# A first transform over 48 rows on quarters of the array, with moved bulk loads, split gate tiles and a new order of work

## The chip, the core and the metric

The kernel runs on one core of a Trainium2 chip. The metric is the device time of one execution in microseconds. The engines are TensorE (PE; PEld is its weight load), VectorE (DVE), ScalarE (ACT), GpSimd (POOL) and SyncE (SP); the last two also issue DMAs.

## The reference, cut to what matters

Three layers in a row. Only the shapes and the steps that the change touches are kept.

```python
x: (8, 3072, 256)                       # batch, sequence, channels
X = np.fft.rfft(x, axis=1)              # over the sequence
Yr = X.real @ w_r - X.imag @ w_i + b_r  # then soft shrinking by 0.01
Yi = X.real @ w_i + X.imag @ w_r + b_i
y = np.fft.irfft(Yr + 1j * Yi, n=3072, axis=1)
...                                     # y as 24576 tokens of 256
logits = y @ phi                        # 32 slots, softmax over all tokens and over the slots
slot_out = mlp_of_8_experts(dispatch.T @ y)
z = combine @ slot_out
...
out = (silu(z @ w_gate) * (z @ w_val)) @ w_out
```

## The kernel before

The program has two phases. Phase 1 is a pipeline over the eight batches, all in one program order; phase 2 is a loop over 576 steps of the gated layer. Between them lies a join: the last batch's logits and slots, the experts' MLP on 32 slots, and the first gate tiles.

**The order.** Phase 1 is a list of tasks. Each `add(engine, fn, ...)` appends a task, with what it reads and writes; `ring` names buffers that take turns. The list `ORDER`, written out by hand, gives the order in which the tasks are emitted: a number is the place of a task in the list, a negative number is the same task given to the second of the two engines that it allows (most often VectorE in place of GpSimd). Each engine works off its own instructions in that order; semaphores between engines, buffers and DMAs are set by the framework. DMAs that SP issues stand in SP's queue in that order too.

**First transform.** A sequence of 3072 is 96 rows (`R1`) times 32 (`R2`). `load_x` brings a quarter of the channels (64) of a batch as a tile "xq" of 96 partitions x 32 x 64, by one DMA on SP; "xq" has two buffers; batch 0 has its own tiles "x0" (`load_first`). `stage_a` takes 16 channels of it: one float32 matmul (L587) of 96 rows x 128 outputs x 512 columns, with the table `fwd` of cosines and sines as weights, into one of two PSUM banks "ac". VectorE turns it by 32 x 32 blocks (L592) into `chan`. There are 16 such matmuls a batch. A float32 matmul shows in the profile as two passes, each with its weight load.

**The rest of a batch.** `stage_c` (L613) does the second step of the transform with the table `cm` (mix), eight passes into a bank "ac", which ScalarE and VectorE split into high and low parts (L629, L632, L635, L638, L647, `sum_lo` L651). `stage_b` (L701) multiplies by the complex weights, `after_b` shrinks (take, gather, relu, `join` L772), `stage_q` (L798) forms the slots' logits on four groups of 32 columns and issues the spreads `yi<-yt` (L827), four DMAs of 64 KB for each of four parts. `logits`, `slots` and `combine` follow, the slots' sums by L1104. `narrow` converts the weights of phase 2 in 18 jobs beside it, through the buffer "cv" (L1202 to L1247).

**The bulk loads.** Near the end of phase 1 `fetch_w1` and `fetch_w2` bring the experts' weights (1 MB for each expert and each matrix) and `fetch_wg` the gate weights into buffers that come free; they stand in SP's or GpSimd's queue among the last spreads. 40 matmuls `hold` (L1391) on an identity fill TensorE while the last logits are made.

**The gate tiles.** `gates(t)` (L1526) multiplies the slots' outputs with a third of w_gate and w_val; `gate_high` (L1532, ScalarE) and `gate_low` (L1537, VectorE) write the high and low parts into one tile `gstk`. `gv(i)` (L1551, L1552) reads 128 columns of it a step; each step has eight matmuls of 512 columns (six of them L1576). `po` (L1464) are the experts' second matmuls.

Of the kernel before, what the change touches and what calls it, by code (L numbers as in the profile page):

```python
# [10 lines left out]
F32 = mybir.dt.float32  # L11
# [21 lines left out]
def dft_tables():  # L33
# [18 lines left out]
    for j in range(NCH):
        for h in range(2):
            if j == 0 and h == 0:
                fwd[:, 0, 0] = 1.0
                fwd[:, 1, 0] = alt1
                for i in range(R2):
                    if i == 0:
                        mix[0, :, j, 0, h, 0] = 1.0
                        continue  # L60
                    src = 0 if i < 16 else 1
# [7 lines left out]
            fwd[:, 2 * h + 1, j] = -np.sin(a)
            a = 2 * np.pi * ((n2[:, None] * (k1[j, h] + 96 * k2)[None, :]) % n) / n  # L70
            mix[2 * h, :, j, 0, h, :] = np.cos(a)
            mix[2 * h + 1, :, j, 0, h, :] = np.sin(a)
            mix[2 * h, :, j, 1, h, :] = -np.sin(a) * sign
            mix[2 * h + 1, :, j, 1, h, :] = np.cos(a) * sign
# [85 lines left out]
for _n, _w in (  # L160
# [11 lines left out]
FWD = 136  # L172
# [191 lines left out]
def kernel(  # L364
# [83 lines left out]
    def phase1():  # L448
# [1251 lines left out]
```

## Time and profile before

| | us |
|---|---|
| median of 3 runs | 1688.4 (1686.91 to 1688.49) |
| the profiled execution | 1691.38 |
| its span in the profile | 1689.5 |

The span is the time from the first to the last instruction of the program in the profile; the execution's own time has 1.9 us around it. "Busy" on TensorE includes the ends of pipelined matmuls, so two neighbours overlap in their records; the distance from start to start tells the pace. "x4" after a line is four passes. In a timeline the brackets hold the idle time of the engine before the group and what ended it. DMA shares and GB/s are those of the 16 DMA engines.

### The profile page before, as it was taken

Reading aid. Unit: us, or ns where it says so; the run is one execution under the profiler, and the core shown is the slowest. Engines: PE = TensorE matmul, PEld = TensorE weight load, DVE = VectorE, ACT = ScalarE, POOL = GpSimd, SP = SyncE. Lnnn points to the kernel's source line nnn. Section 1 sums busy time; section 2 is a strip of 40 time slices with the busy share of each in tenths; the row PEclk is TensorE's granted clock in tenths of the full one; section 3 lists DMA queues with packets and bytes.
Section 4 is the critical chain, followed back from the end, with each engine's and each line's share of the span. In section 5 each row is a group of like instructions: output and inputs, shape, how many; then the busy total and the mean of one; then the engine's idle time right before and its main releaser. Section 6 shows DMA issues by size and latency. Waiting matters only on the chain.

```text
span 1689.5 us, 23317 instructions
## 1 busy us (share of the span) xinstructions
PE 1661.4 (98%) x8186; PEld 1283.0 (76%) x8186; DVE 1307.2 (77%) x2220; ACT 979.2 (58%) x1830; POOL 288.1 (17%) x336
## 2 busy tenths in 40 slices
PE   7999999999999899999999999999999999999998
PEld 4677776776767558888888888888888888888886
DVE  5889888888888458778777777777777777877776
ACT  3655654655656256656666666656656655665564
POOL 1333333334333321100200200200010110110000
PEclk9999999999999999999999999999999999999999
DMA  9477566666658871311310311311231131131111
GB/s 193 93 133 151 106 129 142 124 130 142 127 130 259 283 173 26 81 26 26 81 23 16 81 25 26 74 34 25 44 63 17 22 81 26 25 72 26 25 26 25
DMA packets 260164, 139.94 MB, mean 83 GB/s; under 512 B 210352, under 2 KB 243856, under 8 KB 260048
## 3 DMA queue, kind: packets, MB, share of 16 engines
q1 hardware_dynamic: 249136, 114.47, 32.9%
q0 software_dynamic: 9856, 23.73, 5.6%
q8 instruction: 65, 1.06, 0.3%
q10 hardware_dynamic: 1056, 0.26, 0.1%
q14 instruction: 51, 0.42, 0.1%
HBM read 72.74 MB, written 40.50 MB: 67 GB/s over the span
## 4 chain that ended last, share of the span: by engine, by line
PE 89%; DMA 3%; DVE 3%; SPq 2%; issue 1%; ACT 1%; POOL 0%; ACTq 0%; DVEq 0%; POOLq 0%
PE o L1576 47%; PE pb L701 9%; PE pg L1551 8%; PE pv L1552 8%; PE ac L587 6%; PE ac L613 4%; SPq L827 2%; DMA yi<-yt 1%; PE ch L798 1%; PE ch L866 1%; PE ch L1104 1%; PE ch L1056 1%; PE ch L1012 1%; DMA cm<-in_moe_w_dram 1%; DMA cv<-in_moe_w_val_dram 1%
## 5 line engine op out<-in xcount | busy, mean ns | idle before, releaser
L1576 PE MATMUL o<-hh,wo 128*128 128x512 f32 x2304 | 722.5, 395 | 0.0
L1556 DVE TENSOR_TENSOR h<-sg,pv 128x512 f32<-128x512 f32 x576 | 393.4, 683 | 247.9 <-ACT sg L1554 244.6
L1554 ACT ACTIVATE sg<-pg 128x512 f32<-128x512 f32 x576 | 344.6, 598 | 413.8 <-PE pg L1551 413.8
L1576 PEld LDWEIGHTS o<-hh,wo 128*128 128x128 f32 x2304 | 434.2, 188 | 100.8
L1576 PE MATMUL o<-hl,wo 128*128 128x512 f32 x1152 | 453.8, 394 | 0.0
L1564 DVE TENSOR_TENSOR hl<-h,hh 128x512 fp32r<-128x512 f32 x576 | 397.5, 690 | 0.1
L1563 ACT ACTIVATE hh<-h 128x512 fp32r<-128x512 f32 x576 | 359.4, 624 | 0.3 <-DVE h L1556 0.2
L1576 PEld LDWEIGHTS o<-hl,wo 128*128 128x128 f32 x1152 | 216.1, 188 | 51.9
L1551 PE MATMUL pg<-cst,gstk 96*128 96x512 f32 x576 | 227.7, 395 | 0.0
L1552 PE MATMUL pv<-cst,gstk 96*128 96x512 f32 x576 | 226.1, 393 | 0.6 <-DVE gstk L1537 0.6
L701 PE MATMUL pb<-xg,whl 128*128 128x512 f32 x576 | 183.1, 443 | 1.5 <-ACT yt L753 1.4
L701 PEld LDWEIGHTS pb<-xg,whl 128*128 128x128 f32 x576 | 104.5, 189 | 49.3 <-issue 25.2
L1552 PEld LDWEIGHTS pv<-cst,gstk 96*128 96x128 f32 x576 | 109.7, 190 | 26.0 <-DVE gstk L1537 0.9
L1551 PEld LDWEIGHTS pg<-cst,gstk 96*128 96x128 f32 x576 | 108.1, 188 | 25.6 <-DVE gstk L1537 0.8
L772 POOL TENSOR_TENSOR yt<-r,yt 128x512 f32<-128x512 f32 x68 | 88.5, 1301 | 191.0 <-ACT yt L763 85.0
L592 DVE STREAM_TRANSPOSE chan<-ac 128x512 f32<-128x512 f32 x128 | 90.1, 709 | 34.1 <-PE ac L587 31.5
L587 PE MATMUL ac<-xq,fwd 96*128 96x512 f32 x224 | 111.7, 601 | 1.3 <-DVE sf L638 0.6
L613 PEld LDWEIGHTS ac<-cm,chan 128*128 128x128 f32 x768 | 100.4, 196 | 12.6 <-issue 5.3
L1612 POOL TENSOR_TENSOR e<-e,rs 96x256 f32<-96x256 f32 x28 | 22.6, 833 | 497.8 <-DVE rs L1609 497.8
L613 PE MATMUL ac<-cm,chan 128*128 128x128 f32 x768 | 104.1, 283 | 0.0
L629 ACT ACTIVATE xg<-ac 128x512 fp32r<-128x512 f32 x96 | 56.9, 595 | 59.7 <-PE ac L613 57.5
L701 PE MATMUL pb<-sg,whl 128*128 128x512 f32 x288 | 87.7, 426 | 0.0
(158 smaller groups left out, 1464.8 us busy)
## 6 DMA issues: line engine op xcount, KB each, us to landing
out_dram<-ob SPq DMA_DIRECT2D x190, 128.0 KB, 2.8
yi<-yt SPq DMA_DIRECT2D x368, 64.0 KB, 2.1
xq<-in_x_dram SPq DMA_DIRECT2D x28, 768.0 KB, 8.2
cst<-c_scr POOLq DMA_DIRECT2D x72, 128.0 KB, 2.9
w2s<-in_moe_w_dram POOLq DMA_DIRECT2D x5, 1024.0 KB, 8.4
chan<-in_moe_w_dram SPq DMA_DIRECT2D x7, 512.0 KB, 6.1
x<-in_x_dram SPq DMA_DIRECT2D x4, 768.0 KB, 10.2
cv<-in_moe_w_gate_dram SPq DMA_DIRECT2D x6, 512.0 KB, 4.0
```

The source lines that it names most:

```text
L587: nc.tensor.matmul(out=pt, lhsT=fwd[:, 8 - 8 * dh:136 - 8 * dh], rhs=T[kq][:, :, d1:d1 + 16], start=True, stop=True)
L592: nc.vector.transpose(out=chan[:, 12 * dh:12 * dh + 16, d0:d0 + 16, :].rearrange("p j d i -> p d j i"), in_=T[ka].rearrange("p n d -> p d n"),
L613: nc.tensor.matmul(out=pt[:, :, q:q + 2, i // 2, :], lhsT=chan[:, 16 * dh + j // 2, :, j % 2], rhs=cm[:, j, :].rearrange("p (c h k) -> p c ...
L701: nc.tensor.matmul(out=pt, lhsT=w[:, dh, m, es], rhs=xx, start=m != 1 and dh == 0 and n == 0, stop=dh == 1 and n == 2, skip_group_check=True,)
L772: e.tensor_sub(out=part(), in0=quarters(T[kr]), in1=part())
L1551: nc.tensor.matmul(out=pg, lhsT=gstk[:, 0, f * 128:(f + 1) * 128], rhs=rhs, start=True, stop=True)
L1552: nc.tensor.matmul(out=pv, lhsT=gstk[:, 1, f * 128:(f + 1) * 128], rhs=rhs, start=True, stop=True)
L1554: nc.scalar.activation(out=sg, in_=pg, func=AF.Silu)
L1556: nc.vector.tensor_mul(out=h, in0=sg, in1=pv)
L1563: nc.scalar.activation(out=hh, in_=h, func=AF.Copy)
L1564: nc.vector.tensor_sub(out=hl, in0=h, in1=hh.bitcast(F32))
L1576: nc.tensor.matmul(out=po_t[0][k], lhsT=w[:, f % 4, k * 128:(k + 1) * 128], rhs=a, start=(f == 0 and m == 0), stop=(f == NF - 1 and m == 2 ...
```

## The change

A sequence is now 48 rows (`R0`) times 2 times 32: partition p of a tile holds 64 places in a row, whose two halves of 32 (c = 0, 1) are loaded apart. The table `fwd` has 48 rows x 64 outputs, laid twice on the partitions (0 to 47 and 64 to 111). In batches 1 to 7 a tile "xq" holds one half c of 128 channels, 64 channels on each of the two groups of partitions, by two DMAs of 384 KB (`load_x`, `load_x2`); "xq" has three buffers. `stage_a` issues four float32 matmuls of 48 rows x 64 outputs x 512 columns: rows from group r, outputs to the half c of the partitions of bank r. It fills both "ac" banks; two VectorE turns follow as before. That is 8 such tasks a batch in place of 16. In batch 0 the loads are halves of the channels (128, 512 bytes in a piece), and `stage_a0` issues two matmuls a task, (r, c) = (0, 0) and (1, 1), into one bank. The mix table's size and `stage_c` to `combine` are unchanged.

The loads of `w2` for experts 2, 3, 4, 5 and 7 and of the gate weights 0 and 1 must now stand behind the last spreads of the last batch, and those of `w2` are SP's. The gate tile is eight tiles, cut at 128, 512 and 1024 columns for each of gate and value; ScalarE and VectorE fill the first two cuts before the first step. `ORDER` is written anew over the shorter list: 7 joins and 12 low parts fewer stand on VectorE, and the work of the last job of `narrow` lies after the last batch's last `stage_b` in part. 40 `hold` matmuls remain.

```diff
+R0 = 48
...
-    k1 = np.array([[j, 23 + j] for j in range(NCH)])
-    k1[0] = (0, 47)
+    k1 = np.array([[j, 48 + j] for j in range(NCH)])
+    k1[0] = (0, 24)
+
+    fwd = np.zeros((R0, 2, 32))
+    mix = np.zeros((2, 2, R2, NCH, 2, 2, R2))
...
+    def put_mix(part, j, c, h, i, v):
+        mix[:, part, :, j, c, h, i] = v.reshape((2, R2) + v.shape[1:])
...
+        if j == 0:
+            fwd[:, 0, 0] = 1.0
+            fwd[:, 1, 0] = alt0
+        else:
+            a = 2 * np.pi * ((m1 * j) % R0) / R0
+            fwd[:, 0, j] = np.cos(a)
+            fwd[:, 1, j] = -np.sin(a)
...
     last = np.zeros((128, 2))
     last[0:32, 0] = alt2
+    last[64:96, 0] = alt2
...
+    first = np.zeros((128, FWD))
+    for r in range(2):
+        first[64 * r:64 * r + R0, 8:] = fwd.reshape(R0, 64)
...
-FWD = 136
+FWD = 72
...
-ORDER = [ ... ]
+ORDER = [ ... ]
...
-            ("xq", 2), ("tt", 2), ("ac", 2), ("xg", 2), ("sf", 2), ("sg", 1), ("pb", 3), ("r", 1), ("yt", 2), ("yi", 4),
+            ("xq", 3), ("tt", 2), ("ac", 2), ("xg", 2), ("sf", 2), ("sg", 1), ("pb", 3), ("r", 1), ("yt", 2), ("yi", 4),
...
-        fwd = apool.tile([R1, FWD], F32, name="fwd")
+        fwd = apool.tile([64 + R0, FWD], F32, name="fwd")
...
-            nc.sync.dma_start(out=fwd, in_=csmall[0:R1, 0:FWD])
+            nc.sync.dma_start(out=fwd, in_=csmall[0:64 + R0, 0:FWD])
...
-        def load_first(dq):
+        def load_first(dh, r):
             def go():
-                T["x0", dq] = t = early.tile([R1, R2, 64], F32, name=f"x0{dq}")
+                if ("x0", dh) not in T:
+                    T["x0", dh] = early.tile([64 + R0, R2, 128], F32, name=f"x0{dh}")
                 nc.sync.dma_start(
-                    out=t, in_=x[0, :, dq * 64:(dq + 1) * 64].rearrange("(p n) d -> p n d", n=R2)
+                    out=T["x0", dh][64 * r:64 * r + R0],
+                    in_=x[0, :, 128 * dh:128 * dh + 128].rearrange("(p h n) d -> h p n d", h=2, n=R2)[r],
                 )
 
             return go
+
...
-        def load_x(b, dq):
+        def half_x(k, r):
+            _, b, dh, c = k
+            d0 = 128 * dh + 64 * r
+            nc.sync.dma_start(
+                out=T[k][64 * r:64 * r + R0],
+                in_=x[b, :, d0:d0 + 64].rearrange("(p h n) d -> h p n d", h=2, n=R2)[c],
+            )
+
+        def load_x(k):
             def go():
-                t = sb(xpool, ("xq", b, dq), [R1, R2, 64], "xq", 2)
-                nc.sync.dma_start(
-                    out=t, in_=x[b, :, dq * 64:(dq + 1) * 64].rearrange("(p n) d -> p n d", n=R2)
-                )
+                sb(xpool, k, [64 + R0, R2, 64], "xq", 3)
+                half_x(k, 0)
 
             return go
 
-        def stage_a(b, p, rank):
-            dq, dd = divmod(p, 4)
+        def load_x2(k):
+            def go():
+                half_x(k, 1)
+
+            return go
+
+        def stage_a0(dq, dd, rank):
             dh, d0 = dq // 2, (dq % 2) * 64 + dd * 16
-            kq = ("xq" if b else "x0", *(b, dq)[b == 0:])
-            kt, ka = ("tt", b, dh), ("ac", "a", b, p)
-            d1 = dd * 16
+            ka = ("ac", "a", 0, 4 * dq + dd)
 
             def mm():
                 pt = bank(ka, [128, R2, 16], "ac")
-                nc.tensor.matmul(
-                    out=pt, lhsT=fwd[:, 8 - 8 * dh:136 - 8 * dh], rhs=T[kq][:, :, d1:d1 + 16], start=True, stop=True
-                )
+                for r in range(2):
+                    rows = slice(64 * r, 64 * r + R0)
+                    nc.tensor.matmul(
+                        out=pt[64 * r:64 * r + 64], lhsT=fwd[rows, 8 - 8 * dh:72 - 8 * dh],
+                        rhs=T["x0", dh][rows, :, d0:d0 + 16], start=True, stop=True, skip_group_check=True,
+                    )
 
             def turn():
                 nc.vector.transpose(
@@ -594,8 +623,43 @@
                     in_=T[ka].rearrange("p n d -> p d n"),
                 )
 
-            add("PE", mm, r=["f", kq, kt], w=[ka], new=[("ac", ka)] + ([("tt", kt)] if p % 8 == 0 else []))
-            add("DVE", turn, r=[ka], w=[(*kt, p)])
+            kt = ("tt", 0, dh)
+            add(
+                "PE", mm, r=["f", kt] + [("x0", dh, r) for r in range(2)], w=[ka], new=[("ac", ka)] + ([("tt", kt)] if d0 == 0 else []),
+            )
+            add("DVE", turn, r=[ka], w=[(*kt, 4 * dq + dd)])
+
+        def stage_a(b, dh, dd, rank):
+            kq = [("xq", b, dh, c) for c in range(2)]
+            kt = ("tt", b, dh)
+            ps = [8 * dh + 4 * r + dd for r in range(2)]
+            ka = [("ac", "a", b, p) for p in ps]
+            d1 = dd * 16
+
+            def mm():
+                pt = [bank(k, [128, R2, 16], "ac") for k in ka]
+                for r, c in ((0, 0), (1, 1), (0, 1), (1, 0)):
+                    rows = slice(64 * r, 64 * r + R0)
+                    nc.tensor.matmul(
+                        out=pt[r][64 * c:64 * c + 64], lhsT=fwd[rows, 8 - 8 * dh:72 - 8 * dh],
+                        rhs=T[kq[c]][rows, :, d1:d1 + 16], start=True, stop=True, skip_group_check=True,
+                    )
+
+            def turn(r):
+                def go():
+                    d0 = 64 * r + d1
+                    nc.vector.transpose(
+                        out=chan[:, 12 * dh:12 * dh + 16, d0:d0 + 16, :].rearrange("p j d i -> p d j i"),
+                        in_=T[ka[r]].rearrange("p n d -> p d n"),
+                    )
+
+                return go
+
+            add(
+                "PE", mm, r=["f", kt] + [(*k, r) for k in kq for r in range(2)], w=ka, new=[("ac", k) for k in ka] + ([("tt", kt)] if dd == 0 else []),
+            )
+            for r in range(2):
+                add("DVE", turn(r), r=[ka[r]], w=[(*kt, ps[r])])
...
             for dq in range(4 * (b == 0)):
-                add("SP", load_first(dq), w=[("x0", dq)])
-            for dq in range(4):
-                if b == 0 and dq == 3:
+                for r in range(2 * (dq % 2 == 0)):
+                    add("SP", load_first(dq // 2, r), w=[("x0", dq // 2, r)])
+                if dq == 3:
                     constants(0)
-                if b:
-                    add("SP", load_x(b, dq), w=[("xq", b, dq)], new=("xq", ("xq", b, dq)))
-                for p in range(4 * dq, 4 * dq + 4):
-                    stage_a(b, p, a0 + p * da)
+                for dd in range(4):
+                    stage_a0(dq, dd, a0 + (4 * dq + dd) * da)
+            for dh in range(2 * (b > 0)):
+                for c in range(2):
+                    k = ("xq", b, dh, c)
+                    t = a0 - 1.0 + (8 * dh + 4 * c) * da
+                    add("SP", load_x(k), w=[(*k, 0)], new=("xq", k))
+                    add("SP", load_x2(k), w=[(*k, 1)])
+                for dd in range(4):
+                    stage_a(b, dh, dd, a0 + (8 * dh + 2 * dd) * da)
...
-            def go(eng):
+            def go(eng="SP"):
...
+        yi_last = yi_keys(last, 1) + yi_keys(last, 2)
...
-            add(both_q, fetch_w2(e), w=[f"w2{e}"], new=(new, f"w2{e}") if new else None, after=behind)
+            add(
+                both_q if e in (0, 1, 6) else "SP", fetch_w2(e), w=[f"w2{e}"], new=(new, f"w2{e}") if new else None, after=behind + ([] if e in (0, 1, 6) else yi_last),
+            )
         for t in (0, 1):
             add(
-                "SP", fetch_wg(t), w=[("wg", t)], new=("yt", ("wg", t)), after=[("ws", i) for i, (_, d) in enumerate(jobs) if len(d) == 1] + [("yt", last, 2, 0, 1)],
+                "SP", fetch_wg(t), w=[("wg", t)], new=("yt", ("wg", t)), after=[("ws", i) for i, (_, d) in enumerate(jobs) if len(d) == 1] + [("yt", last, 2, 0, 1)] + yi_last,
             )
...
-        gstk = wp.tile([R1, 2, FD], F32R, name="gstk")
+        cuts = ((0, 0, 128), (0, 128, 512), (1, 0, 512), (2, 0, 512))
+        gst = {(c, m): wp.tile([R1, cuts[c][2] - cuts[c][1]], F32R, name=f"gst{c}{m}") for c in range(4) for m in range(2)}
+
+        def gate_cols(m, f):
+            c, k = ((0, 0), (1, f - 1), (2, f - 4), (3, f - 8))[(f > 0) + (f > 3) + (f > 7)]
+            return gst[c, m][:, k * 128:k * 128 + 128]
...
-        def gate_high(t, m):
-            nc.scalar.activation(
-                out=gstk[0:64, m, t * 512:(t + 1) * 512], in_=pq[t][64 * m:64 * m + 64], func=AF.Copy
-            )
...
-
-        def gate_low(t, m):
+        def gate_high(c, m):
+            t, a, e = cuts[c]
+            nc.scalar.activation(out=gst[c, m][0:64], in_=pq[t][64 * m:64 * m + 64, a:e], func=AF.Copy)
+
+        def gate_low(c, m):
+            t, a, e = cuts[c]
             nc.vector.tensor_sub(
-                out=gstk[64:96, m, t * 512:(t + 1) * 512], in0=pq[t][64 * m:64 * m + 32],
-                in1=gstk[0:32, m, t * 512:(t + 1) * 512].bitcast(F32),
+                out=gst[c, m][64:96], in0=pq[t][64 * m:64 * m + 32, a:e], in1=gst[c, m][0:32].bitcast(F32)
             )
 
         h_t, hs_t, po_t, ob_t = {}, {}, {}, {}
@@ -1548,8 +1626,8 @@
             rhs = cst_t[b, q][:, rh * 512:(rh + 1) * 512]
             pg = ps.tile([128, 512], F32, tag="g", name="pg")
             pv = ps.tile([128, 512], F32, tag="v", name="pv")
-            nc.tensor.matmul(out=pg, lhsT=gstk[:, 0, f * 128:(f + 1) * 128], rhs=rhs, start=True, stop=True)
-            nc.tensor.matmul(out=pv, lhsT=gstk[:, 1, f * 128:(f + 1) * 128], rhs=rhs, start=True, stop=True)
+            nc.tensor.matmul(out=pg, lhsT=gate_cols(0, f), rhs=rhs, start=True, stop=True)
+            nc.tensor.matmul(out=pv, lhsT=gate_cols(1, f), rhs=rhs, start=True, stop=True)
             sg = hp.tile([128, 512], F32, tag="sg", name="sg")
             nc.scalar.activation(out=sg, in_=pg, func=AF.Silu)
             h = hp.tile([128, 512], F32, tag="h", name="h")
@@ -1645,12 +1723,14 @@
             b, at = divmod(i, per)
             if at == 0:
                 jobs = rest_c(b + 1) if b + 1 < B else {}
-            for t, m in {0: ((0, 0), (0, 1)), 1: ((1, 0),), 2: ((1, 1),), 4: ((2, 0),), 5: ((2, 1),)}.get(i, ()):
-                if i == 0 and m == 0:
-                    gates(0)
-                    gates(1)
-                gate_high(t, m)
-                gate_low(t, m)
+            if i == 0:
+                gates(0)
+                gates(1)
+            for c, m in {
+                0: ((0, 0), (0, 1), (1, 0), (1, 1)), 1: ((2, 0),), 2: ((2, 1),), 4: ((3, 0),), 5: ((3, 1),),
+            }.get(i, ()):
+                gate_high(c, m)
+                gate_low(c, m)
             if i < n:
                 gv(i)
             if i == 1:

```

## Rows read from the trace of the kernel before

**Rows 1.** The page, part 1: busy us of each engine, share of the span, instructions.
```profile
PE 1661.4 (98%) x8186; PEld 1283.0 (76%) x8186; DVE 1307.2 (77%) x2220; ACT 979.2 (58%) x1830; POOL 288.1 (17%) x336
```

**Rows 2.** Stretches: start:end, length, busy us by engine, granted clock, DMA share, GB/s.
```profile
30.00:551.00 521.00, 516.67 (x3020) 374.66 (x3020) 446.96 (x801) 306.32 (x615) 176.14 (x165) 1.00 0.65 140
...
615.00:1689.00 1074.00, 1068.12 (x4600) 866.21 (x4599) 818.92 (x1318) 651.05 (x1178) 83.24 (x125) 1.00 0.21 40
```

**Rows 3.** Chain of waits from 30 to 551 us, shares by line.
```profile
by line: PE pb L701 29.4%; PE ac L587 16.5%; PE ac L613 13.6%; SPq L827 3.7%; PE ch L798 3.4%; PE ch L866 3.1%; PE ch L1056 2.3%; PE ch L1104 2.3%; issue 2.2%; PE ch L1012 2.0%; DMA cm<-in_moe_w_dram 2.0%; DMA cv<-in_moe_w_val_dram 1.8%; PE
```

**Rows 4.** Waits of TensorE, 30 to 551 us (total, times, longest); first of five.
```profile
PE pb L701 <- ACT yt L753: 1.4, 2, 1.1
...
```

**Rows 5.** Pieces of the chain of waits in order of time (start, us, what).
```profile
53.14 1.72 PE ac L587 x4
...
308.71 1.88 PE ac L613 x16
...
552.64 1.75 PE ch L1104 x31
...
569.72 14.56 DMA yi<-yt
...
594.45 1.86 PE po L1464 x32
...
608.31 0.60 ACT gstk L1532
...
608.93 0.69 DVE gstk L1537
```

**Rows 6.** Timeline of TensorE, gate matmuls and second phase's first (start, us; idle in brackets).
```profile
606.32 3.65 PE L1526 MATMUL pq<-wg,tail 128*64 128x512 f32 x16 [0.38 <-DVE tail L1509]
...
611.02 0.50 PE L1552 MATMUL pv<-cst,gstk 96*128 96x512 f32 x1 [0.60 <-DVE gstk L1537]
```

**Rows 7.** Timeline of TensorE around a group of column parts in the pipeline.
```profile
313.38 1.10 PE L613 MATMUL ac<-cm,chan 128*128 128x128 f32 x8
314.40 0.64 PE L798 MATMUL ch<-yt,phis 128*32 128x256 f32 x8
314.97 0.97 PE L701 MATMUL pb<-xg,whl 128*128 128x512 f32 x3
```

**Rows 8.** Groups of instructions of VectorE: busy us, mean ns, idle before.
```profile
L592 DVE STREAM_TRANSPOSE chan<-ac 128x512 f32<-128x512 f32 x128 | 90.1, 709 | 34.1 <-PE ac L587 31.5
...
L772 DVE TENSOR_TENSOR yt<-r,yt 128x512 f32<-128x512 f32 x28 | 20.0, 713 | 3.9 <-ACT yt L763 3.2 <-ACT r L763 0.4
...
L651 DVE TENSOR_TENSOR sg<-sf,sg 128x256 fp32r<-128x256 f32 x29 | 14.5, 505 | 0.2 <-ACT sg L647 0.2
```

**Rows 9.** Timeline of SP: issues of spreads.
```profile
494.77 10.32 SPq L827 DMA_DIRECT2D yi<-yt  x16
...
553.62 4.12 SPq L827 DMA_DIRECT2D yi<-yt  x4
...
565.76 4.73 SPq L827 DMA_DIRECT2D yi<-yt  x6
```

**Rows 10.** DMA issues: KB each, median us from issue to landing.
```profile
yi<-yt SPq DMA_DIRECT2D x368, 64.0 KB, 2.1
xq<-in_x_dram SPq DMA_DIRECT2D x28, 768.0 KB, 8.2
```

**Rows 11.** Timeline of TensorE, first x (30 passes are 15 matmuls).
```profile
8.34 16.55 PE L587 MATMUL ac<-x,fwd 96*128 96x512 f32 x30 [8.34 <-DMA fwd<-in_csmall_dram]
```

**Rows 12.** Timeline of TensorE, the last slot matmuls.
```profile
581.01 2.79 PE L1104 MATMUL ch<-yi,p 128*32 128x256 f32 x24 [4.71 <-DMA w2s<-in_moe_w_dram]
584.41 1.74 PE L1104 MATMUL ch<-yi,p 128*32 128x256 f32 x16 [0.62 <-DMA yi<-yt]
```

**Rows 13.** Two stretches of 5 us in the join.
```profile
570.00:575.00 5.00, 5.00 (x40) 4.48 (x39) 4.01 (x9) 0.65 (x2) 1.68 (x3) 1.00 1.05 266
...
580.00:585.00 5.00, 3.37 (x32) 1.54 (x36) 0.00 (x0) 0.00 (x0) 1.80 (x1) 0.50 0.52 194
```

More of the change, by code (lines that the diff above doesn't have):

```diff
@@ L41, in dft_tables @@
     n1 = np.arange(R1)
+    m1 = np.arange(R0)
+    m2 = np.arange(2 * R2)
     n2 = np.arange(R2)
@@ L45, in dft_tables @@
     alt1 = np.where(n1 % 2 == 0, 1.0, -1.0)
+    alt0 = np.where(m1 % 2 == 0, 1.0, -1.0)
     alt2 = np.where(n2 % 2 == 0, 1.0, -1.0)
-    k1 = np.array([[j, 23 + j] for j in range(NCH)])
-    k1[0] = (0, 47)
-    fwd = np.zeros((R1, 4, 32))
-    mix = np.zeros((4, R2, NCH, 2, 2, R2))
-    for j in range(NCH):
+    k1 = np.array([[j, 48 + j] for j in range(NCH)])
[4 more added lines that the diff above has]
+        mix[:, part, :, j, c, h, i] = v.reshape((2, R2) + v.shape[1:])
@@ L53, in dft_tables @@
+    every = slice(None)
+    for j in range(NCH):
+        if j == 0:
[5 more added lines that the diff above has]
+            fwd[:, 1, j] = -np.sin(a)
         for h in range(2):
             if j == 0 and h == 0:
[L55 to L61, printed above, removed]
+                put_mix(0, j, 0, h, 0, np.ones(2 * R2))
+                for i in range(1, R2):
@@ L62, in dft_tables @@
                     k = 96 * i if i < 16 else 48 + 96 * (i - 16)
-                    a = 2 * np.pi * ((n2 * k) % n) / n
-                    mix[src, :, j, 0, h, i] = np.cos(a)
-                    mix[src, :, j, 1, h, i] = -np.sin(a)
+                    a = 2 * np.pi * ((m2 * k) % n) / n
+                    put_mix(0, j, 0, h, i, np.cos(a))
+                    put_mix(0, j, 1, h, i, -np.sin(a))
                 continue
-            a = 2 * np.pi * ((n1 * k1[j, h]) % R1) / R1
-            fwd[:, 2 * h, j] = np.cos(a)
@@ L69, in dft_tables @@
[L69 to L74, printed above, removed]
+            a = 2 * np.pi * ((m2[:, None] * (k1[j, h] + 96 * k2)[None, :]) % n) / n
+            if j == 0:
+                put_mix(1, j, 0, h, every, np.cos(a))
+                put_mix(1, j, 1, h, every, -np.sin(a) * sign)
+                continue
@@ L76, in dft_tables @@
+            put_mix(0, j, 0, h, every, np.cos(a))
+            put_mix(1, j, 0, h, every, np.sin(a))
+            put_mix(0, j, 1, h, every, -np.sin(a) * sign)
+            put_mix(1, j, 1, h, every, np.cos(a) * sign)
     kn = 2 * np.pi * (np.outer(k2, n2) % R2) / R2
@@ L138, in pad @@
         return z
+    first = np.zeros((128, FWD))
+    for r in range(2):
+        first[64 * r:64 * r + R0, 8:] = fwd.reshape(R0, 64)
     small = np.concatenate(
         [
-            pad(np.concatenate([np.zeros((R1, 8)), fwd.reshape(R1, 128)], 1), R1),
+            first,
             pad(gf.reshape(R1, 128), R1),
```

242 rows, old and new, of the table ORDER are left out of this document.

## The prediction

> **What bounds the kernel now.** I read the page first, its engine sums [rows 1]: TensorE is busy 98% of the span, VectorE 77% as the next. A sum over stages with different limits decides nothing, so I cut the span with the view of stretches [rows 2]: the pipeline over the eight batches (30 to 551 us) has TensorE busy for 516.67 of 521 us and VectorE for 446.96 (86%); the second phase (from 615) keeps TensorE busy for 1068 of 1074 us; between them lies the join, where it idles. The granted clock is 1.00 in both stretches. The chain of waits of the pipeline says what is worth saving there [rows 3]: the first transform (L587) is 16.5% of it. TensorE's waits in the pipeline are five groups, 1.4 us the largest, and no x tile is among them [rows 4]. So: the second phase (about 1074 us) is not touched but for its first gate tiles; TensorE time saved in the pipeline is time saved as long as VectorE keeps up; the join has its own limit.
>
> **First transform, batches 1 to 7.** Before, 16 matmuls of 96 rows x 512 columns per batch, each in two passes. Four passes in a row are 1.72 us of the chain, so a pass takes 0.43 us and a matmul 0.86 [rows 5]. 7 x 16 = 112 of them: 96 us. After, four matmuls of 48 rows x 64 outputs, one on each quarter of the array, do what two did: 7 x 8 = 56 groups of eight passes. What must be known is how many of the eight passes run beside each other.
> Columns do. In the gate matmuls (L1526), with two halves of the columns, 16 passes of 512 columns take 3.65 us; one after another they would take 16 x 0.43 = 6.9, in pairs 3.44 [rows 6]. The logits' matmuls (L798) on four column groups: eight passes of 256 columns in 0.57 us until the next kind starts (314.40 to 314.97), against 8 x 0.215 = 1.72 one after another and 0.43 four abreast [rows 7].
> Changing between the whole array and parts costs a little. L613's eight passes last 8 x 0.1175 = 0.94 us by their run of 16 [rows 5], and the L798 group starts 1.02 us after their start: 0.08 in. Out: 0.57 - 0.43 = 0.14. Together 0.22 us [rows 7].
> Whether two groups of rows run beside each other no row shows; the trace has no pair of such matmuls. Bounds: all four at once, 2 x 0.43 + 0.22 = 1.08 us a group, or the two row groups in turn, 4 x 0.43 + 0.22 = 1.94. Against 1.72 that is -0.64 or +0.22, times 56: -36 or +12 us. I take -36, because column groups, the nearest row, overlap without any visible loss.
> The page "TensorE: Matmul & The Clock Gate" of the Trainium skill (Part 3, Measured speedup vs the span model) gives 3.07 times for four row groups; as an estimate by it a group would be 4 x 0.86 / 3.07 + 0.22 = 1.34 us, the saving 21 us and the sum below 1666. No run here shows that figure.
>
> **What the saving runs into.** A group now fills both banks of "ac" at once, and VectorE must turn both (0.709 us each [rows 8]) before the next group may start. I counted the new order, task by task with the durations above: of 37 places where one group follows another with no other user of "ac" between, 28 have between 0.85 and 1.8 us of other TensorE work, where the two turns alone need 1.42. So a late VectorE is felt there. It gets relief: by the signs in the new order 7 joins (0.713 us) and 12 low parts (0.505) go from VectorE to GpSimd, 11 us, and four longer ones, some 4 us [rows 8]; GpSimd, at 176 of 521 us now [rows 2], has the room. VectorE: (447 - 15) / (521 - 36) = 89%, from 86%. At 0.2 us for each of the 28 places I put 6 us of stalls; bounds 0 and, at one VectorE operation (0.69 us) each, 19. Sum of the pipeline: -36 + 6 = -30.
>
> **x loads.** Eight DMAs of 384 KB a batch for four of 768: the same bytes, and 28 more issues on SP, at the 0.65 us that a spread's takes [rows 9], in a queue that holds 3.7% of the chain [rows 3]. The third buffer helps; but a group needs two whole tiles, and the second of the next half can be loaded only after the last group of this one. The order leaves 10 to 13 us of TensorE work there; a load lands in 8.2 [rows 10]. Before, the same distance (four matmuls' tile to the one after next) was 10 to 13 us too, and no wait for x shows [rows 4]. Price 0; bound +2 us for each of 7 batches if SP, whose spreads keep it 10 us at a time [rows 9], comes late.
>
> **The first x.** 512-byte pieces for 256. TensorE starts at 8.34, when the table and the first quarter are there, and has done 15 of 16 matmuls by 24.9 [rows 11]. After, two loads must land before the start, and two constant loads and the weights lie ahead of the second half. I see neither gain nor loss beyond 2 us. Its 16 pairs of quarter matmuls lie on the diagonal: at 0.86 a pair beside each other, as before.
>
> **The join.** SP issues the last spreads, held up among the big w2 loads, until 570.5 [rows 9]; the last takes 14.56 us to land [rows 5] where 2.1 is the median [rows 10]. TensorE, done with the last logits, waits 4.71 and 0.62 us in the slot matmuls [rows 12], its granted clock falls to 0.50, the level of 1.2 GHz, in the idle time [rows 13], and the last 40 of them take 2.79 + 1.74 us, where a run of 31 takes 1.75 elsewhere [rows 5]: 2.26 for 40. So 4.71 + 0.62 + 2.27 = 7.6 us are there. With the bulk behind, SP's 16 issues of 0.65 us (the first goes at 553.62 [rows 9]) end near 564 and land by 566, ten us before the slot matmuls at 576. Next late: six w2 loads of 1 MB and 0.5 MB of stores now start near 565. At the 266 GB/s of a crowded stretch [rows 13] or some more, the fifth ends between 583 and 587 (5.8 MB from 565) and the sixth 3 us later; the expert matmuls (594.45 before [rows 5], 587 after) first need experts 2 and 3, second and fifth in the queue, and the rest some 6 us later. It just fits. SP also holds the last store of the narrowed weights between those loads, and its work now lies on VectorE inside the chain of the last logits: two operations of a join's length. I take -7; bounds -8 and +3.
>
> **Gate tiles.** Before, the first value matmul waits (to 611.02 [rows 6]) for two rounds of ScalarE then VectorE, 0.60 + 0.69 us each from 608.31 on, one behind the other [rows 5]. A round of 128 columns takes between a quarter of 1.29 us and all of it, one of 384 between three quarters and all; with a fixed part I take 0.6 and 1.05. The first cut is then ready at 609.5, before TensorE's gate matmuls are done (606.32 + 3.65); but the second cut's two rounds follow in the same alternation and end near 611.6, when the second step's value matmul asks. The wait moves one step on. Price 0; bounds -1.1 and +0.5.
>
> **Sum.** -30 - 7 = -37. The profiled execution took 1691.38 us (span 1689.5); the median of the runs is 1688.4, and I take the sum from that: 1651.
>
> **Rivals.**
> A. Row groups take turns. A group costs 1.94 us for 1.72 (+12), a diagonal pair of the first x 1.72 for the 1.1 that each of 15 matmuls takes from 8.34 to 24.9 [rows 11] (16 x 0.62 = +10), the join -7: 1688.4 + 15 = 1703. For it: no row shows the overlap. Against: halves and quarters of the columns are shown to be independent. With these terms it is slower than before from a group of 1.67 us on.
> B. VectorE and the two banks take half of the saving: 28 places at 0.69 us, 19 us instead of 6: 1664. For it: 89% and work that is handed over in pairs. Against: at 86% TensorE idled 4 us in 521.
> C. The first x's pairs write the same bank from two row groups, which may not go together: the same +10: 1661. The page "TensorEngine Tiling (Array Packing)" of the Trainium skill (Restrictions and Gotchas, Gotcha 1) says that different row tiles cannot access one PSUM bank at the same time; the later x has a bank for each row group, the first x has not. No row shows such a pair, and here the two also lie on different columns.
> D. The late bulk makes the experts wait: the join gains nothing or loses 3 us: 1658 to 1661.
>
> **How the numbers follow.** Forecast 1651 (1638 to 1661): 0.62. B 0.16 (1661 to 1678), C 0.06, D 0.08, A 0.08. The upper end 1678 takes in B, C and D with some mixing; below 1638 all bounds would have to fall right together; A is left out. So 1638 to 1678. About 0.2% (3.4 us) is what a measurement of this kernel can tell: faster 0.90, within it 0.02, slower 0.08.
>
> **What would show it.** Groups of eight passes with four starting within some 30 ns and 1.0 to 1.1 us until the next kind; 1.9 means A. The pipeline some 30 us shorter with VectorE near 89%; TensorE waiting for the turns means B. First-x matmuls about 1 us apart (C: 1.7). Spreads landing in 2 to 4 us, no wait in the slot matmuls, w2 landing before the expert matmuls. The second phase still at 1074 us. I am wrong if four quarters do not run at once, or if x tiles appear as releasers of TensorE.

## The result and the profile after

The changed kernel takes 1702.0 us (median of 5 runs, 1697.25 to 1706.78) against 1688.4: ratio 1.0076, 95% interval 1.0058 to 1.0094. It is slower by 13.6 us where 37 us of gain were forecast. Its profiled execution took 1702.0 us, its span 1700.1. The profiled execution of the kernel before lies 3 us above its median, so the spans below differ by 10.6 us and the medians by 13.6.

I cut both spans at the same points of TensorE's work: the first complex multiplication (L701, after L765), the last batch's first matmul on `qt` (L866, L930), the fold of the slots' sums (L1424, L1497), the first gate matmul (L1526, L1605), the first output matmul (L1576, L1654) and the end. The last three columns are kernels of the experiments below.

| stretch, us | before | changed | a_wide2 | b_rows | b_bulk |
|---|---|---|---|---|---|
| start to the first multiplication | 28.6 | 43.7 | 43.7 | 29.5 | 29.2 |
| pipeline, to the last `qt` | 526.9 | 527.3 | 504.3 | 537.0 | 526.9 |
| last logits and slots | 31.3 | 23.7 | 23.7 | 26.6 | 23.7 |
| experts | 19.5 | 21.9 | 23.5 | 20.8 | 19.5 |
| first gate tiles | 8.5 | 8.8 | 8.8 | 8.5 | 8.5 |
| second phase | 1074.7 | 1074.6 | 1074.7 | 1074.6 | 1074.5 |
| span | 1689.5 | 1700.1 | 1678.8 | 1697.0 | 1682.2 |

So the first x costs 15.1 us, the pipeline gains nothing at all, and the join gives 7.6 us of which the experts take 2.4 back. The stretches of the changed kernel, as in [rows 2] (start:end, length, busy us of PE, PEld, DVE, ACT, POOL, granted clock, DMA share, GB/s):

```profile
7.00:17.00 10.00, 0.00 (x0) 0.00 (x0) 0.00 (x0) 0.00 (x0) 0.00 (x0) 1.00 1.24 122
...
30.00:551.00 521.00, 504.02 (x3212) 337.85 (x3213) 428.61 (x766) 300.93 (x603) 192.29 (x181) 0.98 0.80 134
...
615.00:1689.00 1074.00, 1072.34 (x4620) 866.38 (x4617) 820.55 (x1323) 657.08 (x1190) 89.89 (x136) 1.00 0.22 43
```

VectorE is busy 82% of the pipeline, less than before; it isn't what holds TensorE up. The DMA engines' share has gone from 0.65 [rows 2] to 0.80 while they move fewer GB/s, 134 for 140: each transfer takes longer. In the first x, from 7 to 17 us, 122 GB/s at a share of 1.24; the kernel before moves 173 GB/s there. The groups of the first transform in the timeline of TensorE (start, us):

```profile
17.10 10.19 PE L615 MATMUL ac<-x,fwd 48*64 48x512 f32 x32 [17.10 <-DMA fwd<-in_csmall_dram]
29.85 9.60 PE L615 MATMUL ac<-x,fwd 48*64 48x512 f32 x28 [2.57 <-DMA x<-in_x_dram]
...
53.52 1.56 PE L765 MATMUL pb<-sg,whl 128*128 128x512 f32 x6
...
70.84 1.09 PE L643 MATMUL ac<-xq,fwd 48*64 48x512 f32 x8
71.86 1.67 PE L765 MATMUL pb<-xg,whl 128*128 128x512 f32 x6
...
264.62 1.08 PE L643 MATMUL ac<-xq,fwd 48*64 48x512 f32 x6
267.57 1.13 PE L643 MATMUL ac<-xq,fwd 48*64 48x512 f32 x2 [1.87 <-DMA xq<-in_x_dram]
```

At 70.84 a group as it should be: 1.02 us to the next kind (71.86), its eight passes in two turns of four that start within 20 ns. 37 of the 56 groups take 1.02 to 1.04 us to the next kind. At 264.62 the last quarter of a group starts 2.95 us behind the others, after an x load. TensorE's waits from 30 to 560 us (what it waited for, total, times, longest), the six groups whose longest is over 1.3 us:

```profile
PE pb L765 <- ACT yt L817: 3.1, 2, 1.8
PE ac L643 <- ACT sg L711: 3.1, 1, 3.1
PE ac L615 <- DMA x<-in_x_dram: 2.6, 1, 2.6
PE ac L643 <- DVE chan L651: 2.1, 2, 1.4
PE ac L643 <- DMA xq<-in_x_dram: 1.9, 1, 1.9
PE ac L677 <- DVE xg L696: 1.4, 1, 1.4
```

Two name x, but behind others the chain of waits has a late DMA: narrow weights (`cv`) that VectorE waits for, spreads that hold a buffer of ScalarE. That chain over the pipeline (44 to 571 us), by line as in [rows 3], where no x load stands among the shares:

```profile
by line: PE pb L765 27.5%; PE ac L643 11.1%; PE ac L677 10.5%; DMA xq<-in_x_dram 7.2%; SPq L891 4.2%; PE ch L1168 3.8%; PE ch L862 3.4%; PE ch L1120 3.3%; DMA yi<-yt 3.0%; PE ch L930 2.6%; issue 2.1%; PE ch L1076 1.8%; DMA w_scr<-cv 1.7%; D
```

After two of these waits, those of 1.87 and 3.1 us, the granted clock was at 0.50, the level of 1.2 GHz, from 268.4 to 271.9 and from 415.2 to 425.5 us (two stretches inside them):

```profile
268.50:271.50 3.00, 3.00 (x6) 1.65 (x6) 0.76 (x2) 0.00 (x0) 0.00 (x0) 0.50 1.01 172
415.50:425.50 10.00, 10.00 (x28) 4.26 (x28) 6.58 (x14) 5.28 (x10) 5.38 (x5) 0.50 0.26 73
```

That is 13.7 us at half the clock, some 7 us of work lost by estimate, which TensorE's idle time does not show. The DMA issues (KB each, median us to landing):

```profile
xq<-in_x_dram SPq DMA_DIRECT2D x56, 384.0 KB, 8.3
x<-in_x_dram SPq DMA_DIRECT2D x4, 768.0 KB, 15.6
cv<-in_moe_w_gate_dram SPq DMA_DIRECT2D x6, 512.0 KB, 6.8
```

Half of the bytes of [rows 10] in the same 8.3 us; the first x's loads 15.6 for 10.2 before; `cv` 6.8 for 4.0 before (5.2 in a_wide2 below, whose x loads are fast, so not all of it is theirs).

### The profile page after: what moved, and what is told of

Its sections match the earlier page's. It is cut to its first block, busy times and chain, and to the rows that moved or that the text cites. A ratio compares the mean times of both kernels' runs of the same rounds, so it can differ in the third digit from the quotient of the medians.

```text
span 1700.1 us, 23840 instructions
## 1 busy us (share of the span) xinstructions
PE 1652.9 (97%) x8442; PEld 1251.7 (74%) x8442; DVE 1294.8 (76%) x2199; ACT 982.0 (58%) x1832; POOL 309.4 (18%) x354
## 4 chain that ended last, share of the span: by engine, by line
PE 87%; DMA 7%; DVE 3%; SPq 2%; ACT 1%; issue 1%; POOL 0%; DVEq 0%; ACTq 0%; POOLq 0%
PE o L1654 47%; PE pb L765 9%; PE pg L1629 8%; PE pv L1630 8%; PE ac L643 3%; PE ac L677 3%; DMA xq<-in_x_dram 2%; SPq L891 1%; DMA x<-in_x_dram 1%; PE ch L1168 1%; PE ch L1120 1%; PE ch L862 1%; PE ch L930 1%; DMA yi<-yt 1%; DMA w2s<-in_moe_w_dram 1%
## 5 line engine op out<-in xcount | busy, mean ns | idle before, releaser
L1654 PE MATMUL o<-hh,wo 128*128 128x512 f32 x2304 | 722.5, 395 | 0.0
L1654 PEld LDWEIGHTS o<-hh,wo 128*128 128x128 f32 x2304 | 434.2, 188 | 100.8
L1654 PE MATMUL o<-hl,wo 128*128 128x512 f32 x1152 | 453.8, 394 | 0.0
L1654 PEld LDWEIGHTS o<-hl,wo 128*128 128x128 f32 x1152 | 216.1, 188 | 51.9
L1629 PE MATMUL pg<-cst,gst 96*128 96x512 f32 x576 | 227.8, 396 | 0.0
L1630 PE MATMUL pv<-cst,gst 96*128 96x512 f32 x576 | 226.1, 393 | 0.6 <-DVE gst L1616 0.6
L765 PE MATMUL pb<-xg,whl 128*128 128x512 f32 x576 | 165.3, 419 | 3.5 <-ACT yt L817 3.1
L765 PEld LDWEIGHTS pb<-xg,whl 128*128 128x128 f32 x576 | 102.9, 191 | 53.8 <-issue 18.0
L1630 PEld LDWEIGHTS pv<-cst,gst 96*128 96x128 f32 x576 | 109.7, 190 | 25.9 <-DVE gst L1616 0.9
L1629 PEld LDWEIGHTS pg<-cst,gst 96*128 96x128 f32 x576 | 108.1, 188 | 26.1 <-DVE gst L1616 1.3
L836 POOL TENSOR_TENSOR yt<-r,yt 128x512 f32<-128x512 f32 x75 | 98.9, 1318 | 151.9 <-ACT yt L827 102.6
L1690 POOL TENSOR_TENSOR e<-e,rs 96x256 f32<-96x256 f32 x28 | 22.6, 833 | 495.8 <-DVE rs L1687 495.8
L651 DVE STREAM_TRANSPOSE chan<-ac 128x512 f32<-128x512 f32 x112 | 73.6, 692 | 20.5 <-PE ac L643 19.8
L699 ACT ACTIVATE sf<-ac 128x256 f32<-128x256 f32 x96 | 36.1, 382 | 86.6 <-PE ac L677 71.4
L765 PE MATMUL pb<-sg,whl 128*128 128x512 f32 x288 | 83.5, 416 | 0.7 <-DVE sg L715 0.4
L715 POOL TENSOR_TENSOR sg<-sf,sg 128x256 fp32r<-128x256 f32 x79 | 58.2, 741 | 136.5 <-ACT sg L711 125.8
## 6 DMA issues: line engine op xcount, KB each, us to landing
w2s<-in_moe_w_dram SPq DMA_DIRECT2D x7, 1024.0 KB, 10.2
x<-in_x_dram SPq DMA_DIRECT2D x4, 768.0 KB, 15.6
```

Source lines behind the costliest of these rows:

```text
L651: nc.vector.transpose(out=chan[:, 12 * dh:12 * dh + 16, d0:d0 + 16, :].rearrange("p j d i -> p d j i"), in_=T[ka[r]].rearrange("p n d -> p ...
L715: e.tensor_sub(out=sview(1), in0=T[ks], in1=sview(0).bitcast(F32))
L765: nc.tensor.matmul(out=pt, lhsT=w[:, dh, m, es], rhs=xx, start=m != 1 and dh == 0 and n == 0, stop=dh == 1 and n == 2, skip_group_check=True,)
L836: e.tensor_sub(out=part(), in0=quarters(T[kr]), in1=part())
L1629: nc.tensor.matmul(out=pg, lhsT=gate_cols(0, f), rhs=rhs, start=True, stop=True)
L1630: nc.tensor.matmul(out=pv, lhsT=gate_cols(1, f), rhs=rhs, start=True, stop=True)
```

## The experiments

Theory ROWS: an x load that writes only partitions 0 to 47, or only 64 to 111, is slow, and delays what stands behind it. Rivals: the number of DMA issues (ISSUES), the number of rows wherever they lie (NUMBER), the new order with its shared banks (ORDER). The kernel before is at 1687.8 to 1688.7 us in all these comparisons. Two loads' rates are compared by landings: in pairs issued within 1 us of each other, how long the shortest first load takes, and how far behind it the second lands (median; the span in brackets).

**b_n and b_rows: the kernel before with its loads cut in two.**

```diff
-                nc.sync.dma_start(
-                    out=t, in_=x[b, :, dq * 64:(dq + 1) * 64].rearrange("(p n) d -> p n d", n=R2)
-                )
+                xs = x[b, :, dq * 64:(dq + 1) * 64].rearrange("(p n) d -> p n d", n=R2)
+                nc.sync.dma_start(out=t[:, 0:16], in_=xs[:, 0:16])
+                nc.sync.dma_start(out=t[:, 16:32], in_=xs[:, 16:32])
```

In b_rows the last two lines are these:

```diff
+                nc.sync.dma_start(out=t[0:48], in_=xs[0:48])
+                nc.sync.dma_start(out=t[48:96], in_=xs[48:96])
```

b_n:

> The kernel before, each later x load (768 KB on partitions 0 to 95) cut into two DMAs of 384 KB along the sequence's inner 32, both on all 96 partitions: as many issues on SP as in the changed kernel, same bytes, same 256-byte pieces. Theory ROWS (the changed kernel's loads are slow because each writes only 48 partitions, 0 to 47 or 64 to 111): packets keep their median of 27 ns, time 1688 +- 2. Theory ISSUES (28 more issues on SP are what costs): SP comes late, x appears as a releaser of TensorE, 1692 to 1705.

b_rows:

> The kernel before, each later x load cut into two DMAs of 384 KB by partitions, 0 to 47 and 48 to 95: same issues and bytes as with the cut along the sequence. Theory ROWS: the packets to partitions 0 to 47 take near 39 ns, as in the changed kernel, and if it is the place and not the number of rows, those to 48 to 95 stay near 27 (the Trainium skill, page SBUF - State Buffer, section Door 1, puts partitions 0 to 63 on one half of the 16 ports and 64 to 127 on the other, so 48 to 95 reach both). The whole load lands 1 to 3 us later; the slack of x before is 1.4 to 10 us, so the time moves by 0 to +6: 1688 to 1694. Theory NUMBER (fewer rows than 96 are slow wherever they lie): both loads near 39 ns. Theory ISSUES: as the cut along the sequence.

Measured: b_n 1687.14 us, ratio 0.9993 (0.9981 to 1.0004). b_rows 1698.53, ratio 1.0065 (1.0044 to 1.0085). The issues and the stretch from 30 to 551 us, of b_n and then of b_rows:

```profile
xq<-in_x_dram SPq DMA_DIRECT2D x56, 384.0 KB, 6.4
...
30.00:551.00 521.00, 517.62 (x3024) 375.23 (x3023) 449.60 (x803) 308.07 (x618) 177.34 (x167) 1.00 0.63 141
```

```profile
xq<-in_x_dram SPq DMA_DIRECT2D x56, 384.0 KB, 7.8
...
30.00:551.00 521.00, 511.07 (x2967) 368.68 (x2966) 436.34 (x789) 300.89 (x607) 174.06 (x165) 1.00 0.74 133
```

Same bytes, pieces and issues: the cut by partitions alone puts the DMA share from 0.63 to 0.74 and costs 10 us, with the old transform. ISSUES falls. NUMBER falls too: in b_rows the first load (0 to 47) takes at least 6.0 us for b_n's 4.1, but the second (48 to 95, 48 rows as well) lands 2.1 us behind the first, as in b_n. It is the place. In the changed kernel, with 0 to 47 and 64 to 111, both loads are slow: 5.5 us at least, and at the ten places where two x loads are issued within 1 us the second lands 3.5 us behind the first (2.9 to 4.6). Where a load to 64 to 111 stands right behind its partner to 0 to 47 (a_adj_x0 below, 20 pairs) it is 3.3 us (2.5 to 4.3). The packets that the expectations speak of agree: from 60 to 500 us an x packet of 256 bytes takes a median of 27 ns before, 26 in b_n, 35 in b_rows, 39 in the changed kernel. The Trainium skill, page SBUF — State Buffer, section "Door 1: The DMA port swizzle", has this rule: partitions 0 to 63 lie on one half of 16 ports, 64 to 127 on the other. These runs agree with it: 0 to 47 and 64 to 111 reach one half each, 48 to 95 reach both. I under-estimated b_rows: it lost 10 us where 0 to 6 were expected.

**a_wide: fast loads under the new transform, first try.**

```diff
-                out=T[k][64 * r:64 * r + R0],
+                out=T[k][0:96, 16 * r:16 * r + 16],
...
-                    rows = slice(64 * r, 64 * r + R0)
+                    rows = slice(64 * r, (R0, 96)[r])
```

> The changed kernel, but each later x load writes 96 partitions (0 to 95) by half of the inner sequence, same 384 KB, same pieces, same number of issues; the second group of rows is 32 rows long (64 to 95), so the first transform of batches 1 to 7 is not the reference's. Theory ROWS: packets back to 27 ns, tiles land 2 to 4 us sooner, the waits inside the groups of quarters (15 us) and behind late weights go: 1670 to 1680 (the first x still costs its 15). Theory ORDER (the new order and the shared banks cost, x only shows it): within 5 us of 1702. Theory ISSUES: the same, 1697 to 1707.

Measured: 1983.87 us. The loads were fast, but the test was spoilt by the second edit: groups of 48 and of 32 rows.

```profile
67.91 4.06 PE L643 MATMUL ac<-xq,fwd 48*64 48x512 f32 x8
71.90 1.68 PE L765 MATMUL pb<-xg,whl 128*128 128x512 f32 x6
```

The eight passes go one after another, 0.5 us each, 4.0 us a group (7.6 in 17 of the 56; the granted clock averages 0.82 from 30 to 551 us). It says nothing on ROWS, so it was made again.

**a_wide2: the same with equal groups.**

```diff
-                out=T[k][64 * r:64 * r + R0],
+                out=T[k][:, 16 * r:16 * r + 16],
...
-                in_=x[b, :, d0:d0 + 64].rearrange("(p h n) d -> h p n d", h=2, n=R2)[c],
+                in_=x.rearrange("b s d -> (b s) d")[(96 * b - 16) * R2:(96 * b + 96) * R2, d0:d0 + 64].rearrange("(p n) d -> p n d", n=R2)[:, 16 * r:16 * r + 16],
```

> The changed kernel, but each later x load writes all 112 partitions of its tile by half of the inner sequence (448 KB in place of 384, 17% more bytes, same pieces of 256 bytes, same number of issues, same groups of 48 rows); the data are blocks of the sequence in another order, so the output is not the reference's. Theory ROWS: the second load of a pair lands some 2.3 us behind the first instead of 4.1, the waits in the groups of quarters go and with them most of the 30 us that the pipeline lost: 1668 to 1682 (the first x still costs its 15). Theory ORDER (VectorE, banks and the new order hold TensorE up, late x only shows it): 1697 to 1707.

Measured: 1679.3 us, ratio 0.9947 (0.9929 to 0.9965): 22.7 us faster than the changed kernel. Issues, stretch, TensorE's two longest waits from 60 to 560 us, and the chain of waits (44 to 548 us):

```profile
xq<-in_x_dram SPq DMA_DIRECT2D x56, 448.0 KB, 5.8
...
30.00:551.00 521.00, 515.77 (x3390) 350.99 (x3391) 445.90 (x795) 314.88 (x627) 205.67 (x195) 0.99 0.67 154
...
PE ch L1040 <- DVE dg L1033: 0.6, 1, 0.6
PE ac L643 <- DMA xq<-in_x_dram: 0.5, 1, 0.5
...
by line: PE pb L765 36.3%; PE ac L677 14.4%; PE ac L643 12.1%; PE ch L862 4.5%; PE ch L1168 4.0%; PE ch L1120 3.4%; PE ch L930 3.2%; PE ch L1076 2.6%; DMA xq<-in_x_dram 2.1%; SPq L891 1.8%; PE ch L990 1.8%; issue 1.1%; DVE sf L702 1.1%; PE 
```

More bytes land sooner (at ten such places the second load lands 2.3 us behind the first, 1.9 to 3.0), the share falls to 0.67, x falls from 7.2% of the chain to 2.1%, TensorE waits nowhere longer than 0.6 us from 60 us on, and the pipeline takes 504.3 us for 527.3. Of these 23 us, 12 are idle time of TensorE (3.9 us of the stretch for 15.9) and some 7 the two falls of the clock, which is granted in full here. New transform, banks and order are the same: ORDER falls. The forecast's 30 us were there but for 7; the x loads took them.

**b_bulk: one part of the change alone, on the kernel before.**

```diff
-            add(both_q, fetch_w2(e), w=[f"w2{e}"], new=(new, f"w2{e}") if new else None, after=behind)
+            if e in LATE:
+                LATE[e] = len(plan.tasks)
+            add("SP" if e in LATE else both_q, fetch_w2(e), w=[f"w2{e}"], new=(new, f"w2{e}") if new else None, after=behind)
...
+        LATE = dict.fromkeys((2, 3, 4, 5, 7))
...
+        late = list(LATE.values())
+        at = 1 + max(n for n, (_, j) in enumerate(order) if j in spreads)
```

The tasks in `late` are put behind place `at` of `ORDER`, the last spread; `fetch_wg` is among them.

> The kernel before with one part of the change alone: the loads of w2 for experts 2, 3, 4, 5 and 7 and of the gate weights stand behind the last spreads in SP's queue, in the order of the experts. By the prediction's step: the slot matmuls start without their waits of 4.71 and 0.62 us and at full clock, -7.6, and the second expert matmul may wait some 2 us, as in the changed kernel: 1680 to 1684. Rival COVER (late w2 gives all of it back at the experts): 1687 to 1691.

Measured: 1683.85 us, ratio 0.9973 (0.9964 to 0.9983); it is faster than both kernels. TensorE's timeline:

```profile
576.67 2.37 PE L1104 MATMUL ch<-yi,p 128*32 128x256 f32 x40
579.71 0.63 PE L1467 MATMUL pst<-fold,acc 128*128 128x32 f32 x4 [0.68 <-DVE acc L1123]
...
587.26 1.93 PE L1507 MATMUL po<-w2s,h1t 128*32 128x256 f32 x32
```

The 40 matmuls of [rows 12] run in one piece at full clock; the stretch of the slots is 31.3 to 23.7, the 7.6 of the prediction. No expert matmul waits: experts 2 and 3 are the first two of the late loads. In the changed kernel their order is 4, 2, 5, then four stores of narrowed weights, then 7 and 3, and there the wait is:

```profile
591.80 2.37 PE L1168 MATMUL ch<-yi,p 128*32 128x256 f32 x40
...
604.80 1.67 PE L1537 MATMUL po<-w2s,h1t 128*32 128x256 f32 x25 [1.86 <-DMA w2s<-in_moe_w_dram]
```

**Repairs that did not repair: second loads through another queue, or sooner.** In a_x0act, a_bothact and a_pool_x0 the second load of a pair goes through another engine's queue (cut; the comments are added here):

```diff
-                nc.sync.dma_start(              # first x: a_x0act, a_bothact, a_adj_x0, a_pool_x0
+                (nc.sync, nc.scalar)[r].dma_start(
...
-            nc.sync.dma_start(                  # later x: a_bothact (a_pool_x0: nc.gpsimd)
+            (nc.sync, nc.scalar)[r].dma_start(
...
+            order.insert(order.index(a) + 1, b) # a_adj_x0: second load right behind the first
```

a_x0act:

> The changed kernel, but the two first-x loads to partitions 64 to 111 are issued by ScalarE, beside SP's two to partitions 0 to 47; nothing else differs. Theory ROWS: both halves of the ports are written at once, the first x's halves land near 13 and 22 us instead of 16.6 and 29.7, and as the pipeline behind waits for its own loads it keeps 5 to 9 us of it: 1693 to 1697. If the pipeline has slack in which a later start is made good: 1700 to 1704.

Measured: 1698.23 us (1693.73 to 1702.32), ratio 1.0062. The pairs land at 13.6 and 22.0 us (16.6 and 29.7 in the changed kernel), and the first multiplication starts 8 us sooner than in the changed kernel:

```profile
13.61 17.92 PE L615 MATMUL ac<-x,fwd 48*64 48x512 f32 x58 [0.34 <-DMA x<-in_x_dram]
...
35.79 1.08 PE L765 MATMUL pb<-xg,whl 128*128 128x512 f32 x3
```

With both halves of the partitions written together the first x lands as fast as before the change (its last part at 21.7 us there). So two queues do give something, against rival ENGINES of a_bothact below. Of the 8 us some 4 are left at the end, less than expected; the runs of either kernel spread over some 9 us, so the 4 is not sharp.

a_bothact:

> The changed kernel, but of each pair of x loads (first x too) the one to partitions 64 to 111 is issued by ScalarE, into another ring, so that both halves of the partitions are written at the same time. Theory ROWS: a pair lands in about 8 us from its first issue, first x's first pair at 10 to 12 us instead of 16.6, its second near 20 instead of 29.7; first x gives back 8 to 12 us and the pipeline 15 to 25: 1662 to 1680, if ScalarE, which now waits for free x buffers in its queue, holds nobody up; up to 10 us more if it does. Rival ENGINES (both rings share the same 16 DMA engines, so nothing is gained): 1695 to 1710.

Measured: 1721.11 us, a miss of the forecast and of the rival. ScalarE's issues mostly come 3 to 25 us after SP's, so only 14 of the 28 pairs overlap at all between issue and landing. Buffers that spreads must empty come free later: ScalarE waits 19.6 us for spreads (5.3 in the changed kernel), GpSimd 19.5 (3.3).

a_adj_x0:

> As the kernel with the first x issued by two engines, and in SP's queue the second load of each later x tile stands directly behind the first (in the changed kernel up to 20 us and 16 spreads lie between). Theory ROWS: the seven tiles that are loaded into a buffer that has just come free land 1 to 5 us sooner; part of the waits in the groups of quarters goes, 5 to 15 us against the kernel with the first x alone: 1680 to 1690. Rival LATENCY (the second load only delays the spreads behind it, which VectorE and ScalarE then wait for): 1692 to 1700.

Measured: 1721.93 us, 24 us above a_x0act; the rival, and worse than it said. The waits for spreads from 60 to 560 us (total, times, longest):

```profile
POOL yt L838 <- DMA yi<-yt: 30.9, 5, 16.1
ACT yt L819 <- DMA yi<-yt: 26.1, 4, 8.7
```

Moving the slow loads ahead in SP's queue does not help: what then stands behind them is waited for sooner than x.

a_pool_x0:

> The changed kernel, of each first-x pair the second load issued by ScalarE (as before), of each later x pair the second by GpSimd, whose queue is a third ring and which stands on the path less than ScalarE. Theory ROWS: where both loads of a pair are on their way together both halves of the ports are written, SP's ring is free of half the x bytes and cv and the spreads land sooner; 1675 to 1695. Rival LATENCY (the two loads of a pair do not meet, GpSimd waits for buffers in its queue and its low parts and joins come late): 1705 to 1730.

Measured: 1707.98 us, ratio 1.0114; the rival again. GpSimd waits 31.7 us for spreads, and again only 14 of the 28 pairs overlap.

**a_k32: why a_wide ran one pass at a time.**

```diff
-                    rows = slice(64 * r, 64 * r + R0)
+                    rows = slice(64 * r, 64 * r + 32)
```

> The changed kernel with 32 rows instead of 48 in each of the four matmuls of the first transform (rows 0 to 31 and 64 to 95; the other 16 rows of each are left out, so the output is not the reference's); loads as in the changed kernel. In the run with 48 rows in one group and 32 in the other all eight passes went one after another, 4.0 us a group for 1.02. Theory UNEQUAL (groups of different length do not run beside each other): groups of 1.02 us, four passes at once, and the time of the changed kernel, 1697 to 1707. Theory SHORT (a group of 32 rows on half the array never does): groups of 4 us and some 1950 to 1990.

Measured: 1702.55 us (one run).

```profile
67.39 1.09 PE L643 MATMUL ac<-xq,fwd 32*64 32x512 f32 x8
68.41 1.66 PE L765 MATMUL pb<-xg,whl 128*128 128x512 f32 x6
```

Four at once again. Groups of unequal length are what did not overlap; why they do not, no run shows.

## Why the prediction was wrong, point by point

- **First transform: right.** A group was to take 1.08 us with its changeover; it takes 1.02 and lengthens the first pass behind it by 0.11 (1.67 for six passes, 1.56 elsewhere): 1.13. Saving 0.59 x 56 = 33 for 36. Four quarters run at once, so rival A's mechanism is refuted. That its 1703 lies next to the measured 1702 is chance: a time alone confirms no mechanism. The Trainium skill, page "TensorE: Matmul & The Clock Gate", Part 3, gives 3.07 times for four row groups; 4 x 0.86 / 1.13 is 3.04 here, for two row and two column groups, which fits if the changeover is within it.
- **What the saving runs into: near.** With fast loads the pipeline gains 22.6 of the 33 us, so 10 go to stalls and the like (not taken apart), where I put 6 (bounds 0 to 19); VectorE is at 86% there (forecast 89%). This includes whatever the 17% more bytes of a_wide2 cost.
- **x loads: this step failed.** I wrote "the same bytes", took 8.2 us from [rows 10] for a load on all 96 partitions, and gave price 0 with a bound of +2 us a batch. But the trace of before had no load on 48 partitions of one half, and I bounded its price by the one load that it does not resemble. The price is 527.3 - 504.3 = 23 us, 3.3 a batch: only in small part from x being awaited by TensorE (1.9 us of its waits name it, the sign of being wrong that I had given), but since the loads in SP's queue land in turn and each x load keeps it some 1.2 us longer (3.5 us behind another load for 2.3), 56 times. Spreads and `cv` behind them come late, ScalarE and VectorE wait, TensorE last, and after two of its waits it ran at half clock. The Trainium skill's page SBUF — State Buffer, "Door 1", had the rule that spoke against the change; I weighed two others.
- **First x: failed, about half of it by the same omission.** "Neither gain nor loss beyond 2 us" for +15.1. Halves instead of quarters must land before the start, and 768 KB land 6.4 to 6.8 us behind the load before (9.8, 16.6, 23.3, 29.7 us), where it was 4.4 to 4.9 before (7.9, 12.8, 17.3, 21.7). Issued in pairs it is 8 us less (a_x0act). The rest was not taken apart; a granted clock of 0.68 from 30 to 40 us (at 0.50 until 36.3) is part of it.
- **Rival C: refuted.** Two matmuls from two groups of rows into one bank start together, 6 to 35 ns apart, and at full clock a pair takes 0.95 us, not 1.72. Here they write different partitions of the bank. The Trainium skill, page "TensorEngine Tiling (Array Packing)", Gotcha 1, says that different row tiles cannot access one PSUM bank at the same time; for different partitions of the bank this trace does not bear that out.
- **The join: right.** -7.6 for -7 in the slots, twice shown (changed kernel and b_bulk). The late bulk costs 1.9 us at expert 3, rival D in small; b_bulk, with experts 2 and 3 in front and no stores between, does not pay it.
- **Gate tiles: right.** +0.3 for 0. The wait moves from [rows 6]'s first step to the second:

```profile
621.05 0.49 PE L1629 MATMUL pg<-cst,gst 96*128 96x512 f32 x1
622.16 0.49 PE L1630 MATMUL pv<-cst,gst 96*128 96x512 f32 x1 [0.62 <-DVE gst L1616]
```

- **The sum.** Span: 15.1 + 0.5 - 7.6 + 2.4 + 0.3 - 0.1 = 10.6 (1689.5 to 1700.1). The medians differ by 13.6.

## What to carry to other kernels

When a change alters which partitions a load writes, its old landing time is no price for it, however equal the bytes: look for a row of a load on those partitions, and where there is none, let the range take in twice the time. A queue that is served in turn passes the delay on to everything behind it, so the engine that waits may name quite another tile; the DMA share of the stretch against its GB/s shows it (0.80 at 134, against 0.65 at 140). Test a suspected load on the old kernel, by a cut that changes nothing but the place: b_n against b_rows settled what the changed kernel's waits did not tell.

## What the runs showed of the hardware

- Loads of 384 KB in 256-byte pieces land behind the load before them in the same queue by 2.1 us (median) when they write partitions 0 to 95 (b_n), or 48 to 95 behind 0 to 47 (b_rows), and by 3.3 us when 64 to 111 behind 0 to 47 (a_adj_x0).
- Loads of 768 KB to 0 to 47 and 64 to 111 land by 16.6 (the first pair) and 29.7 us (the second) through one queue, by 13.6 and 22.0 us when SP and ScalarE issue the two of a pair within 1 us of each other (a_x0act).
- Four matmuls of 48 rows x 64 columns on the array's quarters run at once (1.02 us for eight passes of 512 columns), also in two row groups into one bank; with 48 rows in one group and 32 in the other they run one after another (4.0 us), with 32 in both at once again (1.02).
